# Buffers of the second transform stage: PSUM tiles in turn, one shared SBUF buffer per block, a third result buffer

## The chip, the cores and the metric

One core of a Trainium2 chip runs the whole program. The metric is the time of one execution on the device in microseconds (us), as the median of several runs. The engines are named as in the profile: PE (TensorE, matrix products; PEld is its weight load), DVE (VectorE), ACT (ScalarE), POOL (GpSimd) and SP (SyncE, which here issues the DMAs).

## The reference

A gated long convolution is followed by two dense layers. All is float32.

```python
def _attn_ref(x, v, pos_emb, w1, w2):
    ...
    h_filt = (np.maximum(pos_emb @ w1, 0.0) @ w2) * window
    u = x * v
    L = 2 * S
    Uf = np.fft.rfft(u, n=L, axis=1)
    Hf = np.fft.rfft(h_filt, n=L, axis=0)
    y = np.fft.irfft(Uf * Hf[None, :, :], n=L, axis=1)[:, :S, :]
    return (x * y).astype(np.float32)

def reference(...):
    x = _attn_ref(...)            # S = 12480 positions, 128 channels
    h = x @ w_in                  # 128 to 2048
    g = (a0 + a1*h + a2*h*h + a3*h*h*h) / (1 + |b0|*|h| + |b1|*h*h + 1e-6)
    x = g @ w_out                 # 2048 to 128
    h = x @ w_in2
    return np.maximum(0.01 * h, h) @ w_out2
```

## The kernel before

The convolution is a Fourier transform in two steps with matrix products. The 128 channels are done in two groups of 64 (`g` 0 and 1). For a group, `first` (L560) multiplies signal and filter with the first-step matrices in 32 calls, each of 4 channels, and ACT copies the result from PSUM to the SBUF tile `A` (L574). Then `second_stage` (L585) walks over the 90 rows of the first step in 23 blocks of 4 (the last has 2). The dense layers follow, from the load of `bt0` (L746) and the loop over `order` (L969) on; the change does not touch them.

A block `b` of the second stage goes through these steps:

- SP loads the block's matrix `mt` (L583), three blocks ahead, into one of four buffers.
- PE forms the spectra of filter and signal in the PSUM tile `xp` (L600, four products, 8 matmul instructions in the trace).
- ACT copies the half of `xp` with the filter to the SBUF view `hc` (L602). DVE multiplies the other half with the real and with the imaginary part of `hc` (L609, two instructions, into `t1` and `t2`).
- POOL forms from `t1` and `t2` a difference (L615), a sum (L616) and the sum of both (L617) in the view `yt`; in the last block of group 1 DVE does this.
- Three blocks later PE multiplies the three rows of `yt` with the inverse matrices into the PSUM tile `gp` (L629, in `inverse`). ACT copies a quarter of `gp` to `g1` (L635), DVE adds `g1` to two others and writes the result view `gs` (L636), and SP stores `gs` to the DRAM tile `bd` (L646).

Each engine takes its instructions in the order in which the code is written, and SP its DMAs too, so a DMA that waits holds up all behind it. `t1` and `t2` exist once each, `hc`, `gs` and `g1` twice, `yt` three times. In PSUM, `xp` takes turns through three tiles (`bank_b`, L445, whose counter it shares with the tiles `ap` of `first`), and `gp` has one tile of its own (`ps_s`), but for two of the last three blocks of group 1.

Other work is woven between the blocks. In group 0, `form_u` (L397) forms the rest of the signal on DVE, one instruction after each of blocks 4 to 15: a product (L400) and two sums or differences (L403), four times. `feed` takes steps of `conv_w` (L509), which converts the weights of the dense layers: L516 and L521, L528, L530, L534 and L539 on DVE, L524 and L518 on ACT, one step after each block from block 11 of group 0 on, two steps between the first stages, and one after each block of group 1 until all is done. The load of the next weights (L504) follows L534.

The inverse of the last three blocks of group 0 is done between the first calls of `first` for group 1 (L710 to L713).

Of the kernel before, what the change touches and what calls it, by code (L numbers as in the profile page):

```python
# [10 lines left out]
F32 = mybir.dt.float32  # L11
# [4 lines left out]
ALU = mybir.AluOpType  # L16
# [14 lines left out]
DG = 64  # L31
NG = D // DG
KB = 4
NB = (K1 + KB - 1) // KB
# [258 lines left out]
def conv_moe_moe(ctx: ExitStack, tc: tile.TileContext, I, out, dbg=None):  # L293
    nc = tc.nc
    pe, act, dve, pool, sp = nc.tensor, nc.scalar, nc.vector, nc.gpsimd, nc.sync
# [19 lines left out]
    with tc.manual_schedule():  # L315
# [12 lines left out]
        em = fc.tile([128, 3, 128], F32, name="em")  # L328
# [8 lines left out]

        wk = kp.tile([128, N2 * DG + 4096], F32, name="wk")
        VIEW = {
            "mt": (512, 4), "hc": (512, 2), "t1": (512, 1), "t2": (512, 1), "yt": (768, 3), "g1": (256, 2), "gs": (512, 2),  # L340
        }
        CONV = {"raw": (1024, 2), "ex": (512, 1), "sc": (512, 1), "w": (512, 2)}
        at = {}
# [14 lines left out]
        def view(t, dims, dt=F32, sub=0):  # L358

            n, k = VIEW[t]  # L360
            i = turns[t] % k
            turns[t] += 1
            return cut(at[t][0], at[t][1] + n * i + sub, dims, dt)
# [81 lines left out]
        def bank_b(dims, name):  # L445

            turn_b[0] += 1
            return ps_b.tile([128, *dims], F32, tag=f"b{turn_b[0] % 3}", name=name)
# [136 lines left out]
        def second_stage(g):  # L585

            mts, yts, stores = dict(early) if g else {}, {}, []

            def load_m(b):
                if b < NB:  # L590
                    mts[b] = view("mt", [KB, 128])
                    fetch_m(mts[b], b)

            def second(b):
                kn = kn_(b)
                en = dve if b == NB - 1 and g else pool
                mt = mts.pop(b)
                xp = bank_b([KB, 2, 2, DG], f"xp{g}_{b}")
                for i in range(kn):
                    pe.matmul(xp[:, i], mt[:, i], A[:, :, b * KB + i], start=True, stop=True)  # L600
                hc = view("hc", [KB, 2, DG])
                act.copy(hc[:, :kn], xp[:, :kn, 0])  # L602
                if b >= 3:
                    after = inverse(b - 3)
                    if b < NB - 1 or not g:
                        after()
                t1, t2 = view("t1", [KB, 2, DG]), view("t2", [KB, 2, DG])
                for t, r in ((t1, 0), (t2, 1)):
                    dve.tensor_tensor(  # L609
                        out=t[:, :kn], in0=xp[:, :kn, 1],  # L610
                        in1=hc[:, :kn, r].unsqueeze(2).to_broadcast([128, kn, 2, DG]), op=ALU.mult,
                    )
                yt = view("yt", [3, KB, DG])
                yts[b] = yt
                en.tensor_tensor(out=yt[:, 2, :kn], in0=t1[:, :kn, 0], in1=t2[:, :kn, 1], op=ALU.subtract)  # L615
                en.tensor_tensor(out=yt[:, 1, :kn], in0=t2[:, :kn, 0], in1=t1[:, :kn, 1], op=ALU.add)  # L616
                en.tensor_tensor(out=yt[:, 0, :kn], in0=yt[:, 1, :kn], in1=yt[:, 2, :kn], op=ALU.add)  # L617
                if b == NB - 1 and g:
                    after()

            def inverse(b, own=True):
                kn = kn_(b)
                yt = yts.pop(b)
                if own:
                    gp = ps_s.tile([128, 4, KB, DG], F32, tag="s", name=f"gp{g}_{b}")
                else:
                    gp = bank_b([4, KB, DG], f"gp{g}_{b}")
                for r in (2, 1, 0):
                    pe.matmul(gp[:, r + (r > 0), :kn], em[:, r], yt[:, r, :kn], start=True, stop=True)  # L629

                def after():
                    gs = view("mt" if g and b > NB - 3 else "gs", [KB, 2, DG])
                    dst = gs[:, :kn].rearrange("p k r d -> p r k d")
                    g1 = view("g1", [KB, DG])
                    act.copy(g1[:, :kn], gp[:, 0, :kn])  # L635
                    dve.tensor_tensor(  # L636
                        out=dst, in0=gp[:, 2:4, :kn],
                        in1=g1[:, :kn].unsqueeze(1).to_broadcast([128, 2, kn, DG]), op=ALU.add,
                    )
                    stores.append((bd[g, :, b * KB : b * KB + kn], gs[:, :kn]))  # L640

                return after

            def store():
                while stores:
                    sp.dma_start(*stores.pop(0))  # L646

            m = len(mts)
            for b in range(m, 3):
                load_m(b)  # L650
                yield
            for b in range(NB):

                if b < 3 and m:
                    load_m(b + m)
                elif b >= m:
                    load_m(b + 3)
                store()
                second(b)
                yield  # L660
            for b in range(NB - 3, NB):
                inverse(b, b == NB - 1 or not g)()
                store()
                yield

# [93 lines left out]
        order, bankof, _ = plan()  # L759
# [269 lines left out]
```

## Time and profile before

| | before |
|---|---|
| runs, us | 1573.25, 1573.32, 1580.24 (median 1573.32) |
| profiled execution, us | 1579.27 |
| span of its trace, us | 1577.5 |
| busy: PE, DVE, POOL, ACT | 97%, 90%, 85%, 83% |
| mean granted clock of TensorE | 0.988 |
| second stage of group 0 (first to last L600) | about 80 to 155 us |
| second stage of group 1 | about 212 to 285 us |
| dense layers | from about 292 us to the end |

The profile is that of one execution; times in its rows are counted from the start of the span. An engine that is busy is not always at work that the end depends on: what a stretch is worth is read from what each engine waits for there. The granted clock is that of TensorE as a share of 2.4 GHz: 1.00 is 2.4 GHz and 0.50 is 1.2 GHz.

### The profile page before, as it was taken

What the parts mean: (1) busy time and instruction counts of PE and PEld (TensorE: products, weight loads), DVE (VectorE), ACT (ScalarE), POOL (GpSimd) and SP (SyncE); (2) the same over time, 40 slices, a digit from 0 to 9 for tenths busy, and PEclk for the clock granted to TensorE, in tenths of its full rate; (3) what the DMA queues carried; (4) which work ended last, traced back from release to release, by engine and by line L of the source; (5) the groups of instructions that cost most, each with busy time, mean ns of one, the idle gap of its engine ahead of it and who ended that gap; (6) DMA issues with size and microseconds to landing.
All of it is one profiled execution on the core that took longest, in us unless ns stands there. A gap on an engine that the chain in (4) does not pass through costs nothing.

```text
span 1577.5 us, 22579 instructions
## 1 busy us (share of the span) xinstructions
PE 1529.1 (97%) x7248; PEld 1051.5 (67%) x7248; DVE 1413.6 (90%) x2387; ACT 1312.8 (83%) x2532; POOL 1338.5 (85%) x1167
## 2 busy tenths in 40 slices
PE   7998899799999999999999999999999999999999
PEld 5976678576666666666666666666666666666665
DVE  6567677599999999999999999999999999999992
ACT  4522543489999999999999999999999999999995
POOL 5066047499999999999999999999999999999993
PEclk9999999699999999999999999999999999999999
DMA  8774755683011110111101100000000000000000
GB/s 221 213 234 127 197 183 171 150 186 69 5 34 35 34 28 10 32 34 34 28 15 27 34 14 7 7 13 13 14 7 7 14 7 7 7 7 1 7 7 13
DMA packets 79709, 88.74 MB, mean 56 GB/s; under 512 B 51728, under 2 KB 59506, under 8 KB 78934
## 3 DMA queue, kind: packets, MB, share of 16 engines
q1 hardware_dynamic: 79590, 87.29, 20.5%
q8 instruction: 57, 0.93, 0.3%
q14 instruction: 62, 0.51, 0.1%
HBM read 66.39 MB, written 20.88 MB: 55 GB/s over the span
## 4 chain that ended last, share of the span: by engine, by line
PE 53%; POOL 21%; DVE 12%; DMA 5%; issue 5%; ACT 3%; SPq 0%; POOLq 0%; DVEq 0%; ACTq 0%
PE o1p L881 12%; POOL wk L917 10%; PE o2p L881 9%; PE h L434 7%; PE h L435 6%; PE h L436 6%; POOL wk L908 4%; POOL wk L910 3%; PE xp L600 3%; PE yP L833 3%; PE ap L568 3%; DVE v L919 3%; PE gp L629 2%; DVE g L932 2%; DVE wk L914 2%
## 5 line engine op out<-in xcount | busy, mean ns | idle before, releaser
L917 POOL TENSOR_TENSOR wk<-wk 128x972 f32<-128x972 f32 (+2 forms) x208 | 469.7, 2258 | 37.6 <-DVE wk L914 36.4
L881 PE MATMUL o1p<-g,u 128*128 128x486 f32 (+2 forms) x832 | 385.5, 570 | 0.9 <-DVE g L932 0.6
L908 POOL TENSOR_SCALAR wk<-wk,pars 128x486 f32<-128x486 f32 (+2 forms) x416 | 312.6, 752 | 23.1 <-DMA xt<-xm 15.0
L919 DVE SCALAR_TENSOR_TENSOR v<-wk,absb,v 128x486 f32<-128x486 f32 (+2 forms) x416 | 296.5, 713 | 5.1 <-ACT v L902 4.5
L881 PE MATMUL o2p<-wk,u 128*128 128x486 f32 (+2 forms) x624 | 296.7, 565 | 0.0
L926 DVE SCALAR_TENSOR_TENSOR v<-v,u 128x486 f32<-128x486 f32 (+2 forms) x416 | 272.9, 656 | 15.9 <-ACT u L924 15.5
L902 ACT ACTIVATE v<-h,absb 128x486 f32<-128x486 f32 (+2 forms) x416 | 262.6, 645 | 17.2 <-DVE g L932 15.4
L914 DVE TENSOR_TENSOR wk<-h,wk 128x486 f32<-128x486 f32 (+2 forms) x416 | 269.9, 649 | 0.7
L929 DVE SCALAR_TENSOR_TENSOR v<-v,u 128x486 f32<-128x486 f32 (+2 forms) x416 | 262.6, 657 | 3.3
L924 ACT ACTIVATE u<-u 128x486 f32<-128x486 f32 (+2 forms) x416 | 253.6, 610 | 6.8
L932 DVE TENSOR_TENSOR g<-wk,v 128x486 f32<-128x486 f32 (+2 forms) x416 | 255.9, 647 | 2.3 <-POOL wk L917 1.0
L900 ACT ACTIVATE wk<-h 128x486 f32<-128x486 f32 (+2 forms) x416 | 238.9, 575 | 21.0 <-PE h L436 16.5
L939 ACT ACTIVATE wk<-h 128x486 f32<-128x486 f32 (+2 forms) x416 | 239.4, 576 | 20.3 <-PE o2p L881 9.6
L922 ACT ACTIVATE u<-v 128x486 f32<-128x486 f32 (+2 forms) x416 | 239.1, 575 | 10.6 <-DVE v L919 2.7
L434 PE MATMUL h<-zh,wh 128*128 128x486 f32 (+2 forms) x416 | 237.9, 572 | 5.5 <-ACT rh L941 2.9
L910 POOL TENSOR_SCALAR wk<-wk,pars 128x972 f32<-128x972 f32 (+2 forms) x208 | 238.6, 1147 | 0.0
L434 PE MATMUL h<-uh,wh 128*128 128x486 f32 (+2 forms) x416 | 230.5, 554 | 1.5 <-DVE wk L914 0.9
L881 PEld LDWEIGHTS o1p<-g,u 128*128 128x128 f32 x832 | 153.3, 189 | 87.6 <-issue 34.8
L615 POOL TENSOR_TENSOR wk<-wk 128x256 f32<-128x256 f32 (+1 forms) x45 | 45.0, 1001 | 136.5 <-DVE wk L609 129.4
L435 PE MATMUL h<-zl,wh 128*128 128x486 f32 (+2 forms) x416 | 159.6, 384 | 0.0
L436 PE MATMUL h<-zh,wl 128*128 128x486 f32 (+2 forms) x416 | 159.3, 383 | 0.0
L436 PE MATMUL h<-uh,wl 128*128 128x486 f32 (+2 forms) x416 | 158.1, 380 | 0.0
(86 smaller groups left out, 2286.9 us busy)
## 6 DMA issues: line engine op xcount, KB each, us to landing
bd<-wk SPq DMA_DIRECT2D x44, 256.0 KB
bt<-bd SPq DMA_DIRECT2D x100, 112.5 KB
wk<-c_m SPq DMA_DIRECT2D x43, 256.0 KB
dt<-c_d SPq DMA_DIRECT2D x25, 344.5 KB
wk<-ws SPq DMA_DIRECT2D x16, 512.0 KB
u<-xu SPq DMA_DIRECT2D x16, 384.0 KB
wk<-vu SPq DMA_DIRECT2D x12, 384.0 KB
xt<-xm SPq DMA_DIRECT2D x13, 243.0 KB
```

What stands on the lines that cost most here:

```text
L434: pe.matmul(dst, w_h, z_h, start=start, stop=False)
L436: pe.matmul(dst, w_l, z_h, start=False, stop=stop)
L881: pe.matmul(o, wo[l][:, f], T.pop((src, n))[:, :w], start=(f == 0), stop=(f == NF - 1))
L902: act.activation(bank("v", n)[:, :w], one("h1"), AF.Abs, scale=kk)
L908: pool.tensor_scalar(out=q, in0=sq, scalar1=a3, scalar2=a1, op0=ALU.mult, op1=ALU.add)
L910: pool.tensor_scalar(out=new("p", n, 2)[:, : 2 * w], in0=T["s", n][:, : 2 * w], scalar1=a2, scalar2=a0, op0=ALU.mult, op1=ALU.add)
L914: dve.tensor_tensor(out=half("nn"), in0=one("h1"), in1=two("q"), op=ALU.mult)
L917: pool.tensor_tensor(out=nn, in0=nn, in1=T["p", n][:, : 2 * w], op=ALU.add)
L919: dve.scalar_tensor_tensor(out=one("v"), in0=two("s"), scalar=bb, in1=one("v"), op0=ALU.mult, op1=ALU.add)
L926: dve.scalar_tensor_tensor(out=one("v"), in0=one("v"), scalar=C1, in1=one("r0"), op0=ALU.add, op1=ALU.mult)
L929: dve.scalar_tensor_tensor(out=one("v"), in0=one("v"), scalar=-2.0, in1=one("r0"), op0=ALU.add, op1=ALU.mult)
L932: dve.tensor_tensor(out=mk("g"), in0=two("nn"), in1=one("v"), op=ALU.mult)
```

## The change

The spectra `xp` take turns through two of the three PSUM tiles of `ps_b`, by the parity of the block; the third goes in turn with that of `ps_s` to the inverses `gp`. DVE writes its products straight into `yt`, which has four rows now and still three buffers; difference, sum and total are formed in place there. `t1` and `t2` are gone. The DVE addition of `inverse(b - 3)` stands after the two products of block `b`, not ahead of them. `gs` has three buffers. `xp` does not move the counter of `bank_b` any more.

```diff
-            "mt": (512, 4), "hc": (512, 2), "t1": (512, 1), "t2": (512, 1), "yt": (768, 3), "g1": (256, 2), "gs": (512, 2),
+            "mt": (512, 4), "hc": (512, 2), "yt": (1024, 3), "g1": (256, 2), "gs": (512, 3),
...
-                xp = bank_b([KB, 2, 2, DG], f"xp{g}_{b}")
+                xp = ps_b.tile([128, KB, 2, 2, DG], F32, tag=f"b{b % 2}", name=f"xp{g}_{b}")
...
-                if b >= 3:
-                    after = inverse(b - 3)
-                    if b < NB - 1 or not g:
-                        after()
-                t1, t2 = view("t1", [KB, 2, DG]), view("t2", [KB, 2, DG])
-                for t, r in ((t1, 0), (t2, 1)):
+                after = inverse(b - 3) if b >= 3 else None
+                yt = view("yt", [4, KB, DG])
+                yts[b] = yt
+                for r in (0, 1):
                     dve.tensor_tensor(
-                        out=t[:, :kn], in0=xp[:, :kn, 1],
+                        out=yt[:, 2 * r : 2 * r + 2, :kn].rearrange("p s k d -> p k s d"), in0=xp[:, :kn, 1],
                         in1=hc[:, :kn, r].unsqueeze(2).to_broadcast([128, kn, 2, DG]), op=ALU.mult,
                     )
-                yt = view("yt", [3, KB, DG])
-                yts[b] = yt
-                en.tensor_tensor(out=yt[:, 2, :kn], in0=t1[:, :kn, 0], in1=t2[:, :kn, 1], op=ALU.subtract)
-                en.tensor_tensor(out=yt[:, 1, :kn], in0=t2[:, :kn, 0], in1=t1[:, :kn, 1], op=ALU.add)
-                en.tensor_tensor(out=yt[:, 0, :kn], in0=yt[:, 1, :kn], in1=yt[:, 2, :kn], op=ALU.add)
-                if b == NB - 1 and g:
+                re, im, both = (yt[:, i, :kn] for i in (0, 2, 1))
+                en.tensor_tensor(out=re, in0=re, in1=yt[:, 3, :kn], op=ALU.subtract)
+                en.tensor_tensor(out=im, in0=im, in1=both, op=ALU.add)
+                en.tensor_tensor(out=both, in0=im, in1=re, op=ALU.add)
+                if after:
                     after()
 
-            def inverse(b, own=True):
+            def inverse(b):
                 kn = kn_(b)
                 yt = yts.pop(b)
-                if own:
-                    gp = ps_s.tile([128, 4, KB, DG], F32, tag="s", name=f"gp{g}_{b}")
-                else:
-                    gp = bank_b([4, KB, DG], f"gp{g}_{b}")
-                for r in (2, 1, 0):
-                    pe.matmul(gp[:, r + (r > 0), :kn], em[:, r], yt[:, r, :kn], start=True, stop=True)
+                pool_, tag = (ps_s, "s") if b % 2 else (ps_b, "b2")
+                gp = pool_.tile([128, 4, KB, DG], F32, tag=tag, name=f"gp{g}_{b}")
+                for r, i in ((2, 0), (1, 2), (0, 1)):
+                    pe.matmul(gp[:, r + (r > 0), :kn], em[:, r], yt[:, i, :kn], start=True, stop=True)
...
-                inverse(b, b == NB - 1 or not g)()
+                inverse(b)()
```

L609 becomes L607, L615 to L617 become L612 to L614, L629 becomes L624, L635 and L636 become L630 and L631, and the store L646 becomes L641.

DVE, blocks 8 to 10 of group 0, before. `xp0_8` is the spectrum of block 8 in group 0, `gp0_6` the inverse of block 6; the brackets name the engines and DMA queues whose progress an instruction waits for.

```order
L609 TENSOR_TENSOR wk_86<-xp0_8_918,wk_86 128x512 [waits DVE_49,Pool_49]
L609 TENSOR_TENSOR wk_86<-xp0_8_918,wk_86 128x512 [waits DVE_49]
L403 TENSOR_TENSOR u1_84<-vl1_771 98x8x64 [waits DVE_49]
L636 TENSOR_TENSOR wk_86<-gp0_6_945,wk_86 128x2x4x64 [waits DMAHW4_49,Activation_49]
L609 TENSOR_TENSOR wk_86<-xp0_9_939,wk_86 128x512 [waits DVE_49,Pool_49]
L609 TENSOR_TENSOR wk_86<-xp0_9_939,wk_86 128x512 [waits DVE_49]
L403 TENSOR_TENSOR u1_84<-vl1_771 98x8x64
L636 TENSOR_TENSOR wk_86<-gp0_7_966,wk_86 128x2x4x64 [waits DMAHW7_49,Activation_49]
```

The same place with the change:

```order
L607 TENSOR_TENSOR wk_86<-xp0_8_918,wk_86 128x4x2x64 [waits PE_49,Activation_49]
L607 TENSOR_TENSOR wk_86<-xp0_8_918,wk_86 128x4x2x64 [waits DVE_49]
L631 TENSOR_TENSOR wk_86<-gp0_5_924,wk_86 128x2x4x64 [waits DMAHW6_49,Activation_49]
L403 TENSOR_TENSOR u1_84<-vl1_771 98x8x64 [waits DVE_49]
L607 TENSOR_TENSOR wk_86<-xp0_9_939,wk_86 128x4x2x64 [waits PE_49,Activation_49]
L607 TENSOR_TENSOR wk_86<-xp0_9_939,wk_86 128x4x2x64
L631 TENSOR_TENSOR wk_86<-gp0_6_945,wk_86 128x2x4x64 [waits DMAHW0_49,Activation_49]
L403 TENSOR_TENSOR u1_84<-vl1_771 98x8x64
```

The product waits for PE and ACT in place of POOL, and the addition of the inverse has moved from behind the instruction of `form_u` (L403) to ahead of it.

PE, from the last block of group 0 into the first stage of group 1, before. `ap1_0_0` is the tile of the first call of `first` for group 1.

```order
L600 MATMUL xp0_22_1209<-A_85,wk_86 128x256
L629 MATMUL gp0_19_1213<-wk_86,em_82 128x256 [waits DVE_49,Pool_49]
L629 MATMUL gp0_19_1213<-wk_86,em_82 128x256 [waits Pool_49] x2
L568 MATMUL ap1_0_0_1231<-f1_80,u1_84 64x180 x8
L629 MATMUL gp0_20_1241<-wk_86,em_82 128x256 [waits DVE_49,Pool_49]
L629 MATMUL gp0_20_1241<-wk_86,em_82 128x256 [waits Pool_49] x2
L568 MATMUL ap1_0_4_1252<-f1_80,u1_84 64x180 x8
L629 MATMUL gp0_21_1262<-wk_86,em_82 128x256 [waits DVE_49,Pool_49]
L629 MATMUL gp0_21_1262<-wk_86,em_82 128x256 [waits Pool_49] x2
L568 MATMUL ap1_0_8_1272<-f1_80,u1_84 64x180 x8
L629 MATMUL gp0_22_1282<-wk_86,em_82 128x128 [waits DVE_49,Pool_49]
```

The same place with the change:

```order
L600 MATMUL xp0_22_1209<-A_85,wk_86 128x256
L624 MATMUL gp0_19_1213<-wk_86,em_82 128x256 [waits DVE_49,Pool_49]
L624 MATMUL gp0_19_1213<-wk_86,em_82 128x256 [waits Pool_49] x2
L568 MATMUL ap1_0_0_1231<-f1_80,u1_84 64x180 [waits DVE_49,Activation_49]
L568 MATMUL ap1_0_0_1231<-f1_80,u1_84 64x180 x7
L624 MATMUL gp0_20_1241<-wk_86,em_82 128x256 [waits Pool_49] x3
L568 MATMUL ap1_0_4_1252<-f1_80,u1_84 64x180 x8
L624 MATMUL gp0_21_1262<-wk_86,em_82 128x256 [waits DVE_49,Pool_49]
L624 MATMUL gp0_21_1262<-wk_86,em_82 128x256 [waits Pool_49] x2
L568 MATMUL ap1_0_8_1272<-f1_80,u1_84 64x180 [waits DVE_49]
L568 MATMUL ap1_0_8_1272<-f1_80,u1_84 64x180 x7
L624 MATMUL gp0_22_1282<-wk_86,em_82 128x128 [waits Activation_49,Pool_49]
```

The order is the same. Two of the three calls of `first` shown wait for DVE now, and the last inverse waits for ACT: `ap1_0_0` takes the tile of `xp0_22`, `ap1_0_8` that of `gp0_20`, and `gp0_22` that of `ap1_0_8`.

## Rows read from the trace of the kernel before

**Rows 1.** A window: busy us of PE, PEld, DVE, ACT, POOL; clock, DMA share, GB/s.
```profile
80.00:120.00 40.00, 38.20 (x171) 31.56 (x170) 27.61 (x43) 11.33 (x23) 28.13 (x34) 1.00 0.77 241
```
**Rows 2.** Chain of work that ended last, group 1: start us, us, what.
```profile
240.27 1.73 PE xp L600 x8
242.00 1.29 PE gp L629 x6
```
**Rows 3.** Timeline around block 6 of group 0: start, duration, instruction, [idle before].
```profile
100.72 1.29 DVE L609 TENSOR_TENSOR wk<-xp,wk 128x512 f32<-128x512 f32 x2 [0.70 <-POOL wk L616]
...
101.54 1.89 PE L600 MATMUL xp<-A,wk 128*128 128x256 f32 x8
101.79 0.37 ACT L635 COPY wk<-gp 128x256 f32<-128x256 f32 x1 [0.89 <-PE gp L629]
101.93 0.68 DVE L403 TENSOR_TENSOR u<-vl 98x512 f32<-98x512 f32 x1
102.16 1.04 POOL L615 TENSOR_TENSOR wk<-wk 128x256 f32<-128x256 f32 x1 [0.66 <-DVE wk L609]
102.53 0.68 DVE L636 TENSOR_TENSOR wk<-gp,wk 128x512 f32<-128x512 f32 x1
...
103.16 0.72 POOL L616 TENSOR_TENSOR wk<-wk 128x256 f32<-128x256 f32 x1
...
103.92 1.29 DVE L609 TENSOR_TENSOR wk<-xp,wk 128x512 f32<-128x512 f32 x2 [0.71 <-POOL wk L616]
```
**Rows 4.** Timeline, start of the second stage of group 0.
```profile
79.64 7.17 PE L600 MATMUL xp<-A,wk 128*128 128x256 f32 x32 [0.91 <-ACT A L574]
...
82.29 1.29 DVE L609 TENSOR_TENSOR wk<-xp,wk 128x512 f32<-128x512 f32 x2 [11.94 <-ACT wk L602]
...
87.94 1.89 PE L600 MATMUL xp<-A,wk 128*128 128x256 f32 x8
```
**Rows 5.** Timeline and a window of 5 us, blocks 14 to 18 of group 0.
```profile
131.64 0.33 SPq L504 DMA_DIRECT2D wk<-ws  x1
...
138.25 0.69 DVE L636 TENSOR_TENSOR wk<-gp,wk 128x512 f32<-128x512 f32 x1 [2.85 <-DMA bd<-wk]
...
140.00:145.00 5.00, 5.00 (x17) 4.08 (x17) 2.69 (x6) 1.49 (x3) 3.65 (x6) 0.66 0.42 142
```
**Rows 6.** Timeline, last block of group 0 into the first stage of group 1.
```profile
154.23 1.03 PE L600 MATMUL xp<-A,wk 128*128 128x256 f32 x4
...
157.19 1.44 PE L568 MATMUL ap<-f,u 98*64 98x180 f32 x16
161.21 2.90 PE L629 MATMUL gp<-wk,em 128*128 128x256 f32 x6 [2.58 <-DVE wk L636]
...
168.40 0.76 ACT L574 COPY A<-ap 128x720 f32<-128x720 f32 x1 [0.95 <-PE ap L568]
...
169.15 12.42 PE L568 MATMUL ap<-f,u 98*64 98x180 f32 x160
```
**Rows 7.** Timeline at 28 us; then by line: count, duration ns min/median/max.
```profile
28.10 1.22 DVE L400 TENSOR_TENSOR wk<-wk,u 98x1024 f32<-98x1024 f32 x1
...
28.26 2.14 POOL L462 TENSOR_TENSOR A<-A 128x492 f32<-128x492 f32 x1 [0.48 <-DVE A L458]
...
L403 DVE TENSOR_TENSOR u<-wk x24: 677/688/1600, 29.3 to 69.7; 98x512 f32<-98x512 f32 x24
...
L462 POOL TENSOR_TENSOR A<-A x11: 1221/1226/2139, 8.0 to 32.4; 128x492 f32<-128x492 f32 x10, 128x328 f32<-128x328 f32 x1
```
**Rows 8.** Timeline of group 1, from block 4 to the end of the second stage.
```profile
221.36 1.97 PE L600 MATMUL xp<-A,wk 128*128 128x256 f32 x8 [1.12 <-DMA wk<-c_m]
...
276.96 1.03 PE L600 MATMUL xp<-A,wk 128*128 128x256 f32 x4
...
283.05 2.43 DVE L636 TENSOR_TENSOR wk<-gp,wk 128x512 f32<-128x512 f32 x4
...
289.92 0.83 SPq L731 DMA_DIRECT2D wk<-bd  x2
```

## The prediction

> **What bounds the kernel now.** I read the windows first, then the chain of waits, then the timeline of a block. The window over the first half of group 0's second stage [rows 1] shows the granted clock at 1.00, DVE and POOL busy for 70% (27.6 and 28.1 of 40 us) and the DMA engines for 77%. No engine but PE is full, and a busy PE proves little, so I look at the waits. The chain of waits in group 1 [rows 2] goes through PE alone: 1.73 us of spectra and 1.29 us of inverses, so no block takes less than 3.02 us. In group 0 a block takes longer, and the timeline shows why [rows 3]: DVE's products start 0.70 after it fell idle, released by POOL's sum L616, since the one `t1` and `t2` must be free; the next pair starts at 103.92, 3.20 later. The loop is: two products (1.21 from the first to the next instruction), about 0.23 to POOL, its difference L615, its sum (0.72), back to DVE. L615 took 1.04 there and not 0.72, beside DVE's L403. So group 0 is bound by a DVE-POOL loop, which the four blocks with L400 lengthen further, and group 1 nearly by PE.
>
> Two more losses are seen. L636 waited 2.85 us for a store to free one of two result buffers; that store stood on SP behind the weight load L504 at 131.64. PE went down to 1.2 GHz for a while after that gap: the window behind it has a granted clock of 0.66 [rows 5]. And at the hand-over to group 1's first stage PE waited 2.58 for L636, because the inverses have one PSUM tile; its next six matmuls took 2.90 in place of about 1.5 [rows 6].
>
> **The change part by part.** An instruction on PE, ACT, DVE or POOL is neither added nor removed; all keep their sizes. DVE's product now writes runs of 64 with strides. L636 writes such an output already and takes 0.68, no more than L403 [rows 3], so I cost this at nothing. POOL's operations in place have the same elements: nothing. PE's spectra have one more wait each; the signals are sent 1.2 us ahead (below), so nothing; the 0.25 that a signal takes [rows 3] would cost 11 in 44 blocks if each came last, and nothing in the cycle below makes it come last.
>
> *The new cycle of a block.* Let T be the start of its spectra. They end at T + 1.73, the inverse of block b - 3 at T + 3.02. The products no longer wait for POOL but for that inverse, which reads the buffer of `yt` they write: T + 3.3 with the 0.25 that ACT shows behind PE [rows 3]. They end at T + 4.6, L636 follows to T + 5.2, and DVE is free for the next pair, due at T + 6.3. What waits for the products is POOL and the spectra of block b + 2, which need their tile at T + 6.04: 1.2 us to spare. POOL, three instructions of 0.72, is done by T + 7.0 to T + 8, and its result is read at T + 10.8. The inverses' two tiles in turn and the third `gs` give each a block more. So PE's 3.02 becomes the bound.
>
> *Start of group 0.* The third spectra now need the first tile back. The first products end at 83.58 [rows 4]; with 0.25 the third spectra start at 83.85, not at 83.1. Then 1.73 + 1.73 + 1.29 lead to block 4 at 88.6, against 87.94: 0.7 lost.
>
> *Blocks 4 to 22.* 18 x 3.02 = 54.4, so block 22 starts at 143.0, where it started at 154.23 [rows 6]. Against this stands a price that I can only bound. L403 and L400 read two SBUF operands, and such an instruction and one of POOL hold each other up: at 28.10 L400 ran, POOL's L462, started at 28.26, took 2.14 and not 1.22, and among the L403 is one of 1.60 beside the median of 0.69 [rows 7]. In the old order DVE's extra work fell into POOL's pause. In the new one L636 goes first, and L403 comes 0.61 behind the products, when POOL has begun at 0.23. If it gets in after POOL's first instruction (0.92 behind the products), a block with L403 needs 1.21 + 0.92 + 0.60 = 2.7 of DVE, one with L400 3.3, and blocks 13 to 15, which convert weights too, 3.3 to 3.9. DVE then falls behind by at most 1.9 at block 15, of which 1.2 is spare: 0.7 lost, block 22 at 143.7. If it gets in only after POOL's second instruction, each costs 0.69 more (the first rival). I take the first, as a waiting instruction found its place after one instruction of the other engine in rows 7. Gain up to block 22: 10.5.
>
> The Trainium skill, page SBUF — State Buffer, section Who interferes with whom, speaks against the change here: a DVE instruction with two SBUF inputs and a GpSimd one that reads SBUF exclude each other, and whoever issues first holds the port for the whole instruction. By it DVE is the one that waits in the new order, as one L403 did in rows 7; it does not say who is next after several GpSimd instructions in a row, and the sums above are by rows alone.
>
> *Hand-over.* Block 22 has half the matmuls: 0.86, then an inverse, 1.29. The first call of the first stage takes the tile of block 22's spectra and so waits for its products: 2.15 + 0.25 + 0.8 + 0.25, about 3.5. Then 1.4, 1.29, 1.4, 1.29, 1.4 (the 1.4 from L568) to 10.3. The last inverse needs the tile of the third call and waits for its copy: 0.25 + 0.76 + 0.25 [rows 6], to 11.5, and 0.7 for itself. The fourth call starts 12.2 after block 22, where before it took 169.15 - 154.23 = 14.9 [rows 6]. Gain 2.7; the two new waits cost 2.5 of what it could be.
>
> *First stages and opening of group 1.* From 169.15 to 221.36 [rows 6, 8] nothing is touched; block 4 waited for its matrix behind a weight load on SP, which stays. Nothing gained or lost.
>
> *Group 1.* Block 4 to 22 took 276.96 - 221.36 = 55.6; at 54.4 the gain is 1.2. From block 22 to the end of the last L636 it took 283.05 + 2.43 - 276.96 = 8.5 [rows 8]. Now the products of block 22 need not wait for POOL, but the inverses of 21 and 22 wait for the additions of 19 and 20: 0.86 + 1.29 + 0.25 + 0.8 for the products, 0.9 for DVE's three operations on half a block (estimate: each under half of the 0.68 of a whole one's), 0.6 for the addition of 19, 0.25, then inverse 21 (1.29), inverse 22 (0.7) and its addition (about 1.1) make 8.1. Gain 0.4. From the last addition to the load of the result at 289.92 I leave 4.4.
>
> *DMAs.* No DMA is added. Blocks 4 to 10 move their 0.5 MB each in 3.02 and not in 3.2 and more [rows 3], beside the signal and weight loads, where the engines were busy for 77% [rows 1]. At the weight load L504 of block 14, SP still holds back the matrix of block 18 and a store; the third `gs` gives a block more, which covers the 2.85 of rows 5 only if the transfers are no slower. Ends: nothing and 2.85; I take 1.4, the middle.
>
> **Sum.** 10.5 + 2.7 + 1.2 + 0.4 - 1.4 = 13.4 us. The profiled execution took 1579.27 (span 1577.5) and would take 1565.9. The median is 1573.32, 6 us less; the rows don't show where a run of that length differs. With the same gain it becomes 1560. If the stalls of rows 5 and 6 are what makes those 6 us, the median gains only 7.5 and becomes 1566. I forecast **1560**.
>
> **Rivals.**
> 1. *DVE waits for two of POOL's instructions.* For it: POOL's first two come back to back (L616 needs nothing of L615). Against: rows 7 show a turn after one. A block with L403 then needs 3.4 on DVE, with L400 4.0, blocks 11 to 15 3.8 to 4.6; from 91.9, the products of block 4, the 12 blocks take 45.8 and six more 20.0, so the products of block 22 start at 157.7 and the fourth call at 167.5. Group 1's gain goes as well. About 2 in all: 1571.
> 2. *Slower: POOL keeps the port for all three.* Then each DVE instruction of `form_u` and of the weight conversion waits another 0.8. That is 18 blocks in group 0 and some 9 in group 1, against the first rival 21 us more: 1592. It decides when a DVE instruction cannot enter in the gap before POOL's third, which waits for the second. Against it: that gap is there in any case.
> 3. *The DMAs set the pace* in blocks 4 to 18, because the saved time has to be moved as well. For it: 77% in rows 1; against it: the window is below its full share even so, and the load three blocks ahead was in time. Half the gain of 10.5 goes, and some more waits come: about 1567.
> 4. *The change does not do what it says*: a wait the code does not show keeps the old loop. Against it: in the order of instructions the product's wait on POOL is gone. 1573.
>
> **Chances.** Forecast 0.62, rival 1 0.20, rival 2 0.06, rival 3 0.09, rival 4 0.03. The range takes in the forecast with both readings of the median and the ends of its terms (1554 to 1567) and rival 1 to 1573: **1553 to 1573**. A change of 0.5%, 8 us, is about what a measurement of this kernel tells from none. Faster by more means below 1565.5: most of the forecast and a little of rival 3, 0.60. Slower by more is rival 2 and a little else, 0.07. The rest, 0.33.
>
> **What would show it.** Right: the products' idle time ends on ACT or PE, not on POOL; spectra starts 3.02 apart in both groups from block 4 on; no wait of the addition on a store; a clock of 1.00 from 80 to 200 us; the fourth call of the first stage near 156; PE idle twice for about 1.2 at the hand-over. Wrong: L403, L400 or L530 with durations above 1 us, and block spacings of 3.4 to 4.6 in blocks 4 to 15 (rival 1), or above 4 (rival 2); spectra that wait for `c_m` (rival 3).

## The result, and the profile after

The changed kernel takes 1559.42 us (median of four runs, 1556.76 to 1559.64) against 1573.62 for the kernel before beside it: a ratio of 0.9896, 95% interval 0.9868 to 0.9924 (the ratios here and below compare all runs of the two kernels, not the two medians). Run again later it took 1558.98 (six runs, ratio 0.9905, 0.9879 to 0.9931). The profiled execution took 1559.5, its span is 1557.7.

The windows over the second stage of group 0 answer to [rows 1] (columns as there):

```profile
80.00:120.00 40.00, 39.68 (x185) 34.55 (x184) 35.29 (x52) 13.21 (x27) 36.06 (x41) 1.00 0.84 261
120.00:160.00 40.00, 36.75 (x249) 31.15 (x249) 32.86 (x56) 17.43 (x33) 24.21 (x29) 1.00 0.52 166
```

In the same 40 us DVE is now busy for 35.29 (27.61 before) and POOL for 36.06 (28.13), and the granted clock stays at 1.00 to 160 us. From 160 to 200 us, where 1.00 had been forecast too, it is 0.96 in this trace and 1.00 in the second one. The chain of waits there is now what [rows 2] showed for group 1, PE alone, 1.73 and 1.29:

```profile
95.07 1.73 PE xp L600 x8
96.80 1.29 PE gp L624 x6
98.10 1.73 PE xp L600 x8
```

The timeline of one block answers to [rows 3] (start, duration, engine, line; L607 is the products, L612 to L614 POOL's three, L631 the addition, L624 the inverse):

```profile
96.39 0.68 DVE L631 TENSOR_TENSOR wk<-gp,wk 128x512 f32<-128x512 f32 x1
96.61 0.73 POOL L612 TENSOR_TENSOR wk<-wk 128x256 f32<-128x256 f32 x1 [0.20 <-DVE wk L607]
96.64 1.46 PE L624 MATMUL gp<-wk,em 128*128 128x256 f32 x6
96.98 0.91 DVE L403 TENSOR_TENSOR u<-vl 98x512 f32<-98x512 f32 x1
97.30 1.18 POOL L613 TENSOR_TENSOR wk<-wk 128x256 f32<-128x256 f32 x1
97.93 1.89 PE L600 MATMUL xp<-A,wk 128*128 128x256 f32 x8
98.20 1.29 DVE L607 TENSOR_TENSOR wk<-xp,wk 128x512 f32<-128x512 f32 x2 [0.31 <-PE gp L624]
98.56 0.73 POOL L614 TENSOR_TENSOR wk<-wk 128x256 f32<-128x256 f32 x1
```

The products wait for the inverse and no longer for POOL; L614 of one block even ends after the next products have begun. Stage by stage, in us (block 4 and 22: the start of their spectra; fourth call: of group 1's first stage; wP: the run of matmuls of L828, before the change L833, that the loaded result releases). The kernel before was traced a second time, as run b_again below, and so was the changed one:

| stretch | before | before, again | after | after, again | forecast |
|---|---|---|---|---|---|
| start to group 0's first spectra | 79.64 | 76.39 | 76.98 | 79.81 | as before |
| first spectra to block 4, group 0 | 8.30 | 8.31 | 8.87 | 8.87 | 9.0 |
| block 4 to 22, group 0 | 66.29 | 64.47 | 55.46 | 55.54 | 56.5 |
| block 22 of group 0 to fourth call | 14.92 | 13.13 | 12.74 | 12.75 | 12.2 |
| fourth call to block 4 of group 1 | 52.21 | 52.70 | 52.62 | 50.43 | 52.2 |
| block 4 to 22, group 1 | 55.60 | 55.31 | 54.47 | 54.47 | 54.4 |
| block 22 of group 1 to wP | 14.89 | 14.46 | 12.80 | 13.15 | 14.5 |
| wP to the end | 1285.65 | 1286.53 | 1283.76 | 1282.68 | as before |

Of the 13.6 us between the spans of columns two and three, 9.0 lie in the blocks of group 0, 0.4 in the hand-over, 0.8 in group 1's blocks, 1.7 behind them and 2.8 in the dense layers; the first two rows give 1.1 back, and the fifth changes by 0.1.

The start answers to [rows 4]: block 4 comes 8.87 behind the first spectra, since the third ones wait for a tile (the profile names no releaser for their 0.32, but the first products, which read that tile, end 0.10 before them).

```profile
76.98 3.72 PE L600 MATMUL xp<-A,wk 128*128 128x256 f32 x16 [0.92 <-ACT A L574]
79.63 1.29 DVE L607 TENSOR_TENSOR wk<-xp,wk 128x512 f32<-128x512 f32 x2 [9.64 <-ACT wk L602]
81.02 3.69 PE L600 MATMUL xp<-A,wk 128*128 128x256 f32 x16 [0.32 <-issue]
85.85 1.89 PE L600 MATMUL xp<-A,wk 128*128 128x256 f32 x8
```

At the place of [rows 5] no addition waits for a store any more. What is left is a wait of block 18's spectra, whose matrix is asked for behind the weight load L504. The first trace names DVE's L516, whose result these spectra don't use (the products that free their tile ended 1.30 before); the second trace names the DMA. First the changed kernel, then its second trace:

```profile
123.46 0.33 SPq L504 DMA_DIRECT2D wk<-ws  x1
129.15 1.97 PE L600 MATMUL xp<-A,wk 128*128 128x256 f32 x8 [0.83 <-DVE wk L516]
```

```profile
132.06 1.96 PE L600 MATMUL xp<-A,wk 128*128 128x256 f32 x8 [0.92 <-DMA wk<-c_m]
```

The hand-over answers to [rows 6]: the wait of 2.58 is gone and two new ones are there.

```profile
141.31 1.03 PE L600 MATMUL xp<-A,wk 128*128 128x256 f32 x4
145.10 1.44 PE L568 MATMUL ap<-f,u 98*64 98x180 f32 x16 [1.47 <-DVE wk L607]
153.22 0.91 PE L624 MATMUL gp<-wk,em 128*128 128x128 f32 x6 [0.95 <-ACT A L574]
154.05 2.20 PE L568 MATMUL ap<-f,u 98*64 98x180 f32 x26
```

The end of group 1 answers to [rows 8]: the load of the result follows the last addition by 2.55 (269.48 to 272.03), where it was 4.44.

```profile
265.65 1.28 DVE L631 TENSOR_TENSOR wk<-gp,wk 128x512 f32<-128x512 f32 x2
268.46 1.02 DVE L631 TENSOR_TENSOR wk<-gp,wk 128x512 f32<-128x512 f32 x2 [1.52 <-ACT wk L630]
272.03 0.83 SPq L726 DMA_DIRECT2D wk<-bd  x2
```

### The profile page after: what moved, and what is told of

It is laid out like the page before. It is cut to its first block, busy times and chain, and to the rows that moved or that the text cites. A ratio compares the mean times of both kernels' runs of the same rounds, so it can differ in the third digit from the quotient of the medians.

```text
span 1557.7 us, 22611 instructions
## 1 busy us (share of the span) xinstructions
PE 1519.0 (98%) x7248; PEld 1047.7 (67%) x7248; DVE 1418.9 (91%) x2387; ACT 1314.1 (84%) x2532; POOL 1344.1 (86%) x1167
## 4 chain that ended last, share of the span: by engine, by line
PE 59%; POOL 19%; DVE 13%; issue 4%; ACT 3%; DMA 2%; SPq 1%; DVEq 0%; POOLq 0%; ACTq 0%
PE o1p L876 12%; PE o2p L876 9%; POOL wk L912 9%; PE h L434 7%; PE h L435 7%; PE h L436 7%; PE xp L600 4%; PE ap L568 4%; POOL wk L903 4%; POOL wk L905 3%; PE gp L624 3%; DVE v L914 3%; PE yP L828 3%; DVE g L927 2%; DVE wk L909 2%
## 5 line engine op out<-in xcount | busy, mean ns | idle before, releaser
L903 POOL TENSOR_SCALAR wk<-wk,pars 128x486 f32<-128x486 f32 (+2 forms) x416 | 315.8, 760 | 19.7 <-ACT wk L895 19.1
L921 DVE SCALAR_TENSOR_TENSOR v<-v,u 128x486 f32<-128x486 f32 (+2 forms) x416 | 273.4, 657 | 13.4 <-ACT u L919 13.0
L435 PE MATMUL h<-ul,wh 128*128 128x486 f32 (+2 forms) x416 | 158.0, 380 | 0.0
```

What stands on the lines that cost most here:

```text
L435: pe.matmul(dst, w_h, z_l, start=False, stop=False)
L903: pool.tensor_scalar(out=q, in0=sq, scalar1=a3, scalar2=a1, op0=ALU.mult, op1=ALU.add)
L921: dve.scalar_tensor_tensor(out=one("v"), in0=one("v"), scalar=C1, in1=one("r0"), op0=ALU.add, op1=ALU.mult)
```

## The experiments

Three parts of the change can be set apart: the shared buffer `yt` (with the sums in place), the two PSUM tiles in turn together with the addition behind the products, and the third result buffer. My theory was the prediction's: the buffer ends the loop between DVE and POOL, and tiles and result buffer take away the waits around it. The rivals were that PE's single tiles were the larger limit, and that much of the gain was only the difference between executions.

| kernel | shared buffer | tiles in turn | addition | result buffers | us | ratio to before, 95% |
|---|---|---|---|---|---|---|
| yt_alone | yes | no | ahead | 2 | 1566.07 | 0.9944 (0.9923 to 0.9964) |
| yt_gs3 | yes | no | ahead | 3 | 1559.81 | 0.9906 (0.9881 to 0.9930) |
| psum_alone | no | yes | behind | 2 | 1575.65 | 1.0008 (0.9994 to 1.0023) |
| psum_old | yes | no | behind | 3 | 1587.32 | 1.0078 (1.0056 to 1.0100) |
| gs_two | yes | yes | behind | 2 | 1560.41 | 0.9915 (0.9891 to 0.9939) |
| add_first | yes | yes | ahead | 3 | 1562.58 | 0.9909 (0.9886 to 0.9931) |
| after | yes | yes | behind | 3 | 1559.42 | 0.9896 (0.9868 to 0.9924) |

**b_again**: the kernel before, unchanged.

> The kernel before, once more, for a second trace. The profiled execution of before took 6 us more than the median. Theory A: the 6 us lie outside the second stages (its span had 2.66 us more ahead of group 0's second stage than the changed kernel, and 1.9 us more behind the last result load). Then an execution near 1573 us still shows blocks 4 to 22 of group 0 in about 66 us and 15 us from block 22 to the fourth call of the first stage. Theory B: the store wait and the slow clock of blocks 17 and 18 make the 6 us: then blocks 4 to 22 take about 60 us in an execution near 1573.

Measured: 1573.09, 6.2 less than the execution that the prediction was made from. By the table above 3.25 of it lie ahead of group 0's second stage, 1.8 in its blocks and 1.8 in the hand-over; the rest nearly cancels. So neither theory came: the blocks took 64.47, not 66 or 60, and the hand-over 13.13, not 15. Most of the last two is TensorE's clock. Behind the store wait the eight matmuls of block 18 took 3.31 in the first trace and 1.89 in this one. The six inverses at the hand-over waited 2.15 and took 1.53 in this one; in [rows 6] they waited 2.58 and took 2.90:

```profile
154.89 0.69 DVE L636 TENSOR_TENSOR wk<-gp,wk 128x512 f32<-128x512 f32 x1 [2.06 <-DMA bd<-wk]
155.73 1.53 PE L629 MATMUL gp<-wk,em 128*128 128x256 f32 x6 [2.15 <-DVE wk L636]
162.30 0.98 PE L568 MATMUL ap<-f,u 98*64 98x180 f32 x10
```

So about 3.6 of the 6 us lay in the blocks and the hand-over, which the change touches, and 3.25 did not.

**yt_alone**: the shared buffer alone.

```diff
- "t1": (512, 1), "t2": (512, 1), "yt": (768, 3), ... "gs": (512, 2)
+ "yt": (1024, 3), ... "gs": (512, 2)
...
- t1, t2 = view("t1", [KB, 2, DG]), view("t2", [KB, 2, DG])
+ yt = view("yt", [4, KB, DG])
```

The products and sums are those of the change; tiles and order are those of before.

> The kernel before with one part of the change alone: products, difference, sum and total share yt; PSUM tiles, order of the addition and two gs stay as before. Theory (the loop of DVE and POOL over t1 and t2 was the bound): spectra 3.02 us apart, blocks 4 to 22 of group 0 in 55 to 59 us (with one store wait of up to 3 us), hand-over still about 13 to 15 us, the whole about 1562 to 1565 us. Rival (the second PSUM tile of the inverses is what makes the gain): blocks stay at 3.2 to 3.7 us, 66 us in all, 1571 us or more.

Measured: 1566.07, over half of the gain. The spectra of group 0 start 3.02 apart except for four slips of 0.2 to 0.4 and one gap of 7.99, in which an addition waits 3.35 for a store, PE waits 3.41 for that addition, and the inverses then run at half clock (2.90):

```profile
125.39 1.89 PE L600 MATMUL xp<-A,wk 128*128 128x256 f32 x8
129.85 0.69 DVE L636 TENSOR_TENSOR wk<-gp,wk 128x512 f32<-128x512 f32 x1 [3.35 <-DMA bd<-wk]
130.69 2.90 PE L629 MATMUL gp<-wk,em 128*128 128x256 f32 x6 [3.41 <-DVE wk L636]
...
133.38 0.93 PE L600 MATMUL xp<-A,wk 128*128 128x256 f32 x2
```

That gap puts blocks 4 to 22 (60.56) and the time just above the ranges that were expected. So the buffer by itself ends the loop; with the tiles of before, PE's 3.02 can be reached.

**gs_two**: the change with two result buffers.

```diff
- "gs": (512, 3)
+ "gs": (512, 2)
```

> The changed kernel with two result buffers in place of three. Theory: spectra stay 3.02 us apart; the addition waits for a store once or twice, 1 to 3 us each, behind the weight loads of blocks 14 and 20; 1 to 4 us slower than the changed kernel, about 1562 us. Rival (the third buffer is the larger part of the gain, as the store wait also took the clock down): 7 us or more slower, 1567 us.

Measured: 1560.41, blocks 4 to 22 in 56.22, within the range that was expected. In this order an addition may be late by a block without holding up PE, as the next inverse goes to the other tile: additions still waited 4.0 us for stores in all, PE for none of them.

**psum_old**: the change with the PSUM tiles of before, the addition still behind the products.

```diff
- xp = ps_b.tile([128, KB, 2, 2, DG], F32, tag=f"b{b % 2}", ...)
+ xp = bank_b([KB, 2, 2, DG], f"xp{g}_{b}")
...
- pool_, tag = (ps_s, "s") if b % 2 else (ps_b, "b2")
- gp = pool_.tile([128, 4, KB, DG], F32, tag=tag, ...)
+ gp = ps_s.tile([128, 4, KB, DG], F32, tag="s", ...)
```

> The changed kernel with the PSUM tiles as before: spectra through three, inverses in one. Theory: the addition now stands behind the products, and the products wait for the inverse, so with one tile the inverse waits for the addition of the inverse before: 1.29 + 0.25 + 1.3 + 0.7 + 0.25 makes about 3.75 us per block in both groups, 25 us slower than the changed kernel, about 1584 us, slower than before. Rival (the PSUM tiles hardly matter): 3.02 us per block, 1560 to 1563 us.

Measured: 1587.32, slower than before. The blocks come 3.67 apart in both groups (65.5 from block 4 to 22 in group 1). The timeline shows a new loop:

```profile
92.40 1.53 PE L623 MATMUL gp<-wk,em 128*128 128x256 f32 x6 [0.41 <-DVE wk L630]
93.77 1.89 PE L600 MATMUL xp<-A,wk 128*128 128x256 f32 x8
94.04 1.29 DVE L607 TENSOR_TENSOR wk<-xp,wk 128x512 f32<-128x512 f32 x2 [0.97 <-PE gp L623]
95.25 0.68 DVE L630 TENSOR_TENSOR wk<-gp,wk 128x512 f32<-128x512 f32 x1
96.07 1.53 PE L623 MATMUL gp<-wk,em 128*128 128x256 f32 x6 [0.41 <-DVE wk L630]
```

The products wait for the inverse, whose input they overwrite; the addition stands behind them; the next inverse waits for the addition, which empties the one tile: 96.07 - 92.40 = 3.67. Buffer and order of this change need the second tile of the inverses.

**psum_alone**: the tiles and the order of the change with the old `t1`, `t2`, `yt` and two result buffers.

```diff
- "yt": (1024, 3), "gs": (512, 3)
+ "t1": (512, 1), "t2": (512, 1), "yt": (768, 3), "gs": (512, 2)
...
- yt = view("yt", [4, KB, DG])
+ t1, t2 = view("t1", [KB, 2, DG]), view("t2", [KB, 2, DG])
+ yt = view("yt", [3, KB, DG])
```

Products and sums are written as in the kernel before.

> The changed kernel without the shared buffer: the products go to the single t1 and t2 again, POOL reads them and writes the sums to the three old yt buffers, and there are two result buffers. The two tiles in turn for spectra and inverses stay, and the addition stays behind the products. My theory is that the loop between DVE and POOL then still sets the block in group 0: products 1.21 to POOL's start 0.23 later, the difference 0.73, L403 between, the sum 1.18 as lengthened by it, 0.05 back to DVE, so 3.2 to 3.5 for a block, blocks 4 to 22 in 60 to 63, and group 1, which has no L403, near 3.02 to 3.2. With the store waits of two buffers where they fall: 1565 to 1571. A rival says that PE's single tiles were the larger part of the limit: then blocks are near 3.02 in both groups, blocks 4 to 22 take 55 to 57, and the time is 1560 to 1562.

Measured: 1575.65, no gain. The forecast blocks came (62.81 from 4 to 22, 56.32 in group 1). The total lies above my range because block 4 came 10.0 behind the first spectra and the hand-over took 17.9, its first call waiting 3.77 and the next inverses running at half clock. The loop is the old one, now 3.33 long with an L403 in it:

```profile
97.48 1.29 DVE L606 TENSOR_TENSOR wk<-xp,wk 128x512 f32<-128x512 f32 x2 [0.62 <-POOL wk L613]
98.92 0.73 POOL L612 TENSOR_TENSOR wk<-wk 128x256 f32<-128x256 f32 x1 [0.66 <-PE gp L624]
99.29 0.91 DVE L403 TENSOR_TENSOR u<-vl 98x512 f32<-98x512 f32 x1
99.60 1.17 POOL L613 TENSOR_TENSOR wk<-wk 128x256 f32<-128x256 f32 x1
100.81 1.29 DVE L606 TENSOR_TENSOR wk<-xp,wk 128x512 f32<-128x512 f32 x2 [0.62 <-POOL wk L613]
```

The rival on the tiles falls: alone they bring nothing in total. Against the second trace of before, group 0's blocks gain 1.7, and its start (1.7) and the hand-over (4.8) lose more.

**add_first**: the change with the addition ahead of the products.

```diff
- after = inverse(b - 3) if b >= 3 else None
+ if b >= 3:
+     inverse(b - 3)()
...
- if after:
-     after()
```

> The changed kernel with one thing undone: a block issues the addition of three blocks earlier ahead of its products again, as the kernel before did. The three buffers, the two tiles in turn and the third result buffer stay. My theory is that the new cycle bears this: with T the start of the spectra, the copy of the inverse's real part ends near T + 3.6, the addition would run to T + 4.6 and the products to T + 5.8, and the spectra that need their tile are due at T + 6.04, so with the 0.25 of a signal nothing is left but nothing is lost: blocks 3.02 apart as in the changed kernel, at most 3.1. L403 would then come right behind the products and ahead of POOL's first operation: I expect it back near 0.68 (it is 0.91 in the changed kernel), and POOL's first operation L612 lengthened in place of its second, L613. Time 1559 to 1562. A rival says that the moved addition is what lets PE go on: then PE waits for the products in each block, by 0.3 or more, and 18 blocks in each group lose 5 us or more each: 1568 and above.

Measured: 1562.58. Blocks 4 to 22 take 55.77 and start 3.02 apart to 118.84, so in the blocks the order of the two is free as long as there are two tiles. L403 falls back only in part (0.68 to 0.91, 0.79 in the mean of eight); the one of POOL's three that is lengthened is now the first, as expected (1.21 in the mean, the second 0.72). The hand-over loses what the time shows: its first call waits 2.23 for the products, the next inverses run at half clock, and the fourth call comes after 15.1.

```profile
145.92 1.44 PE L568 MATMUL ap<-f,u 98*64 98x180 f32 x16 [2.23 <-DVE wk L608]
147.29 2.93 PE L623 MATMUL gp<-wk,em 128*128 128x256 f32 x6
```

**yt_gs3**: the kernel before with the shared buffer and three result buffers.

```diff
- "t1": (512, 1), "t2": (512, 1), "yt": (768, 3), ... "gs": (512, 2)
+ "yt": (1024, 3), ... "gs": (512, 3)
```

> The kernel before with the shared buffer and a third result buffer; the PSUM tiles and the place of the addition stay as they were before. In the run with the shared buffer alone the blocks of group 0 started 3.02 apart but for three slips of 0.2 to 0.4 and one gap of 5.0 at block 18, where the inverse waited 3.41 for an addition that waited 3.3 for a store. My theory is that the third result buffer covers that store, as the second PSUM tile of the inverses does in the changed kernel with two result buffers: blocks 4 to 22 take 55 to 57 (60.6 with the shared buffer alone), the fourth call comes 12 to 13 after block 22, and the time is 1560.5 to 1562.5, within 3 us of the changed kernel. What the two tiles in turn bring would then be small here. A rival says that the single PSUM tile holds PE up at block 18 whatever the result buffers are, as the addition of block 15 stands behind DVE's conversion work: then block 18 still loses 2 us or more and the time is 1564 to 1566.

Measured: 1559.81, the time of the whole change. Block 18 waits 0.30, blocks 4 to 22 take 55.76, and the hand-over takes 10.94, not the expected 12 to 13: with three tiles in turn the first call finds its tile free. So the two tiles bring nothing to the total that these runs can tell. They cost 0.56 at the start (8.87 against 8.31) and 1.8 at the hand-over, and give back about 1 us behind group 1's block 22. There DVE still makes the last four additions in a row, and the load follows 4.14 behind them:

```profile
264.73 2.43 DVE L636 TENSOR_TENSOR wk<-gp,wk 128x512 f32<-128x512 f32 x4
271.30 0.83 SPq L731 DMA_DIRECT2D wk<-bd  x2
```

**tiles_handover**: the change with other tiles for three calls.

```diff
- ap_ = bank_b([4, 256], f"ap{g}_{s}_{c}")
+ if g and not s and i < 3:
+     ap_ = ps_b.tile([128, 4, 256], F32, tag=f"b{(i + 1) % 2}", ...)
+ else:
+     ap_ = bank_b([4, 256], f"ap{g}_{s}_{c}")
```

> The changed kernel, but the first three calls of group 1's first stage take the tiles b1, b0, b1 in place of b0, b1, b2, so that b2 is left to the last inverses and the first of these calls finds its tile free. My theory is that the two new waits at the hand-over cost what they show, 1.47 us for the first call and 0.95 for the last inverse in the changed kernel's trace: both go, the fourth call starts 10.2 to 10.8 after block 22 (12.7 now), and the kernel takes 1557 to 1558. A rival says that the addition of block 20, with DVE's weight conversion in front of it, ends last there whatever the tiles are: then the wait only moves to the inverse of block 22, the hand-over stays near 12.5 and the time at 1559 to 1560. A wait of call 3 for the copy of call 1 (they share b1 now) is what could take back part of it: at most 0.5.

Measured: 1555.70, ratio 0.9876 (0.9854 to 0.9898). Both waits are gone and the fourth call comes 10.21 after block 22, a gain of 2.5. The time lies below the expected range by another 1.3, which isn't explained: the traced execution reaches group 0's second stage 2.5 earlier than the first trace of the changed kernel, at a place that the edit doesn't touch.

```profile
139.11 1.03 PE L603 MATMUL xp<-A,wk 128*128 128x256 f32 x4
141.36 1.44 PE L571 MATMUL ap<-f,u 98*64 98x180 f32 x16
148.46 0.94 PE L627 MATMUL gp<-wk,em 128*128 128x128 f32 x6
149.32 0.98 PE L571 MATMUL ap<-f,u 98*64 98x180 f32 x10
```

**load_later**: the change with the next weight load issued one step later.

```diff
- load_w(c + 2)
  yield
  dve.scalar_tensor_tensor(out=w, in0=w, ...)
...
+ load_w(c + 2)
  yield
```

> The changed kernel, but each weight conversion issues its next weight load one step later, behind its last operation instead of behind the one before it. My theory is that the wait of block 18 for its matrix (0.83 in the changed kernel's trace) comes from that load standing ahead of the matrix on SP: with the load one block later the wait of block 18 falls under 0.3, and blocks 4 to 22 take 54.4 to 55.0 (55.5 now), if no later matrix is caught in its place. Time 1558.5 to 1559.5. A rival says that the transfers share their engines in any order: then one block from 18 to 20 still waits 0.8 or more, and nothing is won. The weight arrives later too: if the first stages of group 1 wait for it, up to 1 us is lost there.

Measured: 1557.82, ratio 0.9884 (0.9869 to 0.9898). Blocks 4 to 22 take 54.39, which is 18 x 3.02 with nothing over: the wait of block 18 was the weight load. The 1.1 of this stage and 0.6 between blocks 0 and 4 of group 1 (8.99, where the changed kernel takes 9.63 and 9.57) are all that is shown; the total's interval overlaps that of the changed kernel.

**later_tiles**: both of these edits.

> The changed kernel with both of the edits that each made it shorter: the first three calls of group 1's first stage take the tiles b1, b0, b1, and each conversion issues its next weight load one step later. My theory is that the two gains lie in different places and add up: blocks 4 to 22 of group 0 in 54.4 (as with the later load alone), the fourth call 10.2 after block 22 (as with the tiles alone), and 50.4 to 50.8 from the fourth call to block 4 of group 1, where the later load took away a wait of block 4 for its matrix. That is 1.1 + 2.5 + 2.0 = 5.6 less than the changed kernel: 1553 to 1555. A rival says that one of them takes the other's gain, since with a faster hand-over the matrices of group 1 are asked for sooner and meet the later weight loads: then block 4 of group 1 waits again for 1 us or more and the time is 1555.5 or above.

Measured: 1555.33, ratio 0.9879 (0.9859 to 0.9899). The stages add up as forecast (54.39 and 10.22), but the time is just above the range: from the fourth call to block 4 of group 1 it takes 51.40, not 50.4 to 50.8 (the changed kernel without these edits had 50.43 in its second trace, so the 2.0 of the sum was not the later load's), and DVE's conversion waits 1.8 for its weights at the hand-over. It can't be told from the tiles alone (1555.70). It and tiles_handover have the lowest times of the study, some 4 us under the changed kernel's median, though the intervals of their ratios overlap with its own.

**after_again**: the changed kernel once more.

> The changed kernel once more, unchanged, in the same stretch of runs as the two others. It gives a second trace and a measure of how far its executions differ. I expect 1557 to 1561; 55.0 to 56.0 for blocks 4 to 22; 12.7 for the hand-over; and from the fourth call to block 4 of group 1 either 50.5 or 52.6, according to whether the matrix of block 4 is late. If the times of the stages ahead of group 0's second stage differ from the first trace by 2 us or more, as the two traces of the kernel before do there, then that part of the difference between executions is not the change's.

Measured: 1558.98. Its trace starts group 0's second stage 2.8 later than the first and reaches block 4 of group 1 in 2.2 less; the span is 1557.7 in both. The 2.2 is not a late matrix of block 4, as I had expected: blocks 0 to 4 take 9.63 and 9.57. It lies in the first stage, whose calls 17 to 32 take 22.77 in the first trace and 20.80 in this one. In the first trace PE waits 2.24 there for a copy of ACT, which stood behind a step of the weight conversion that waited for its weights, and the clock falls (0.96 from 160 to 200 us). Such shifts ahead of and between the second stages come and go without the change.

## Why the prediction was right, and where not

- **The cycle of 3.02**: right, in both groups, and within 0.1 for 18 blocks where no matrix is late (54.39 and 54.47, against 54.4). L631 waits for no store, as forecast.
- **What makes it**: half right. I gave the tiles and the third result buffer each a share; yt_gs3 shows that the buffer and the third result buffer are enough; gs_two shows that the tiles can stand in for the third result buffer. Only one of the two is needed, and the second tile of the inverses is needed where the addition stands behind the products (psum_old).
- **The port, 0.7**: the mechanism held and the price was nothing. DVE's L403 gets in after POOL's first instruction; by line, from 80 us on, first the changed kernel and then the second trace of the kernel before (busy us, mean ns):

```profile
L613 POOL TENSOR_TENSOR wk<-wk 128x256 f32<-128x256 f32 x22 | 28.2, 1281 | 0.0
L403 DVE TENSOR_TENSOR u<-vl 98x512 f32<-98x512 f32 x8 | 7.3, 908 | 0.0
L400 DVE TENSOR_TENSOR vl<-vl,u 98x1024 f32<-98x1024 f32 x4 | 5.8, 1441 | 0.0
```

```profile
L403 DVE TENSOR_TENSOR u<-vl 98x512 f32<-98x512 f32 x8 | 5.4, 681 | 0.0
L400 DVE TENSOR_TENSOR vl<-vl,u 98x1024 f32<-98x1024 f32 x4 | 4.9, 1216 | 0.0
```

  Each pays 0.23 there, and load_later, which has the same rows, loses nothing in 18 blocks. What was mis-sized is how far DVE falls behind: 1.2 at most, not 1.9 (the products of block 16 start 4.48 behind their spectra, those of an undisturbed block 3.29), and the 1.2 us to spare just cover it. The exclusion that the Trainium skill states (SBUF — State Buffer, Who interferes with whom) is seen: DVE waits for POOL's first, and POOL's second for DVE. The first rival, a wait of DVE for two of POOL's instructions, is not seen, nor the second.
- **Start, 0.7 lost**: 0.56 measured.
- **DMAs, 1.4**: 1.07 (55.46 against 54.39), by half of the mechanism named: the matrix of block 18 was late behind L504, and load_later takes that away. The 2.85 that the term was bounded by was a store wait, and of that nothing is left.
- **Hand-over, 2.7 gained**: mis-sized. The end was forecast well (12.2, measured 12.74; the two new waits 2.42 together), but it was set against the 14.92 of one execution. Against 13.13 in the second trace the gain is 0.4. [rows 6] showed the half clock, 2.90 in place of 1.53, and I priced it as lasting.
- **Group 1's end, 0.4 gained and "4.4 to the load" left as it was**: failed. To the end of the last addition the gain is 0.2 (8.5 before, 8.3 now). From the last addition to the load it takes 2.0 to 3.0 in each of the eight traces that have the two tiles in turn, and 4.1 to 4.4 in the four with the old tiles and the old order. psum_old, with the old tiles and the addition behind the products, has 2.7, and add_first, with the tiles in turn and the addition ahead, 2.0, so either of the two is enough. What these nine share is that the last four additions no longer come in a row; that their four stores at once make the difference is argued, not shown.
- **The dense layers, unchanged**: 2 to 4 shorter beside the two traces of the kernel before. Over the thirteen traces this stretch lies between 1282.5 and 1286.5; the two of before (1285.7 and 1286.5) and add_first (1285.2) are the longest, and psum_alone, which gains nothing, has 1282.5. Most of it lies just behind wP, where TensorE starts at half clock and in those three gets back to 2.4 GHz later: DVE's first forty instructions there take 26.3 to 26.8, in the other ten 23.1 to 24.2. The windows from 10 to 20 us behind wP show it, first the second trace of before, then the changed kernel (columns as in [rows 1]; add_first has a clock of 0.59, the others 0.80 to 0.93):

```profile
294.77:304.77 10.00, 10.00 (x65) 8.64 (x62) 5.49 (x14) 5.81 (x15) 5.58 (x7) 0.51 0.80 185
283.94:293.94 10.00, 9.21 (x89) 7.66 (x87) 7.67 (x20) 8.04 (x21) 7.85 (x10) 0.82 0.84 188
```

  Why the clock comes back later in these three stays open; add_first has the shared buffer, the two tiles and the third result buffer.
- **Profile and median**: I took the gain of the profile, 13.4, off the median. Against the profile of before 19.8 was measured, against the second trace 13.6. That the total came so near is luck in part, as errors cancel: against the second trace the forecast has 2.3 too much at the hand-over and 1.0 in the blocks, 4.0 too little behind group 1's block 22 and in the dense layers, and leaves out 0.6 that was lost ahead of group 0's second stage.

## What to carry to other kernels

A buffer that a slower engine must read empty before the next block may be written is a loop; giving the two steps one shared buffer of three, with the sums in place, ended it here with no more memory for them, while more PSUM tiles alone brought nothing. An instruction moved behind another on a queue may close a new loop through its output's tile (3.67 where 3.02 was possible), so walk round every ring of buffers once in the new order. Trace the kernel before twice before pricing a stall that a dip of the clock follows.

## What the runs showed of the hardware

- A DVE instruction with two SBUF operands that meets three POOL instructions one after the other gets in after the first: L403 takes 0.91 and not 0.68, and POOL's second, L613, 1.18 and not 0.73 (its first, L612, stays at 0.73). Where two of DVE's follow one another (L400 and L530 at 118.16 in the changed kernel), L613 takes 2.31.
- At the hand-over PE's next work ran at 1.2 GHz after some waits and not after others: the inverses took 2.90 after 2.58 idle in the kernel before, 1.53 after 2.15 in its second trace, and 2.93 in add_first after a wait of 2.23 and a call that still took 1.44 (granted clock over these inverses 0.52, 1.00 and 0.50). Between the first two, 0.43 more of waiting came with 1.37 more in the matmuls behind it.
- Behind PE's wait for the loaded result (4.3 to 6.5 us idle in the thirteen traces) the granted clock was 0.50 from 5 to 10 us behind wP in all of them; from 15 to 20 us it was 1.00 in ten and 0.52 to 0.68 in three.
